# Reading direction and byte positions of matmul operands in an attention and gated-MLP kernel

## The chip, the cores and the metric

The kernel runs on one core of one Trainium2 chip. The metric is the device time of one execution, in microseconds (us). A profile of one execution stands beside it; its span runs from the first to the last instruction.

## The reference

The input x has 2048 rows of 512. It is layer-normalised, and the result goes two ways. One is attention with 32 heads of 16 columns, in which each row looks at 8 earlier rows, two apart; the other is a two-layer MLP with a hidden width of 1792 and a squared ReLU. The MLP's output, through a SiLU, gates that of the attention.

```python
xn = _layernorm(x, axis=-1)
# attention: qkv = xn @ wqkv; each row attends to rows s, s-2, ..., s-14; then @ wo
s = _A_ref(xn, A_wqkv, A_wo)
# MLP: h = relu(xn @ w1 + b1) ** 2; out = h @ w2 + b2
g = _silu(_B_ref(xn, B_w1, B_b1, B_w2, B_b2))
return x + s * g
```

## The kernel before

**The products.** TensorE does four kinds of product, and each of them is a run of matmuls of a 128x128 stationary operand, which a weight load brings in, with a moving operand of 512 columns. All operands are split into a high and a low float32r part, and each product is the sum of three passes (PASSES, line 34): high by high, high by low, low by high. So a product over 512 rows of input is 4 x 3 = 12 matmuls into one PSUM bank. Every matmul has a weight load of its own.

- `qkv` (line 477) makes q, k and v: the stationary operand is a part of xt, the normalised and transposed x of one tile of 128 rows; the moving operand is a row block of wqkv (`wq`). In the profile: `pq<-wq,xt`, or `pq<-wq,xT` for the first four tiles, which lie in xT.
- `up` (line 509) makes one block of 128 hidden columns for a chunk of 512 rows: stationary w1 (in `w12[f]`), moving four pieces of 128 columns of x. In the profile: `ph<-xT,w` for the first chunk, `ph<-xU,w` for the others, whose x parts are read back from memory.
- `down` (line 653) multiplies h by w2: stationary 128 columns of h, moving 512 columns of w2, which lies in the same buffer as w1. For each of four tiles of 128 rows, three matmuls are added into the bank `pb[j]`. In the profile: `pb<-w,h`.
- `out_product` (line 689) multiplies the attention's output by wo: stationary oT, moving wot. In the profile: `pw<-wot,oT`.

**The stages.** First the weights and the first tiles of x are loaded and split. Then comes the qkv stage, tile pair by tile pair (lines 598 to 645), in which VectorE begins the attention, which it computes without TensorE. Then come four chunks of 512 rows (lines 721 to 817): for each f, one `up` of 12 matmuls and one `down` of 12, with out products and the gate in between. The attention runs along on VectorE; two running sums of estimated time, one for TensorE and one for VectorE (`clock`, line 57), decide while the program is built how much of it is put between two products. Each engine's instructions are kept in the order in which they are written.

**Where the operands lie.** A tile's place in a partition follows from the sizes of the tiles before it. In the kernel before, the parts that are read as moving operands (wq, w12, xT, xU, wot) all begin 480 bytes past a multiple of 512, and so do the stationary parts in w12, h, oT and xT: one matmul's stationary part is 128 float32r numbers, 512 bytes, and parts follow each other in whole multiples of 512 bytes. Only the tiles xt (`place`, line 444; buffers of pool pxT), which are the stationary operands of `qkv` from the fifth tile on, begin 384 bytes past a multiple of 512. Below, the distance of a matmul is the place of the stationary part that is loaded while it runs, less the place where its moving operand begins, modulo 512 bytes. It is 416 in those `qkv` products and 0 in nearly all others.

Of the kernel before, what the change touches and what calls it, by code (L numbers as in the profile page):

```python
# [8 lines left out]
F32 = mybir.dt.float32  # L9
FR = mybir.dt.float32r  # L10
# [4 lines left out]
P = 128  # L15
# [37 lines left out]
def body(ctx: ExitStack, tc: tile.TileContext, x, wqkv, wo, w1, b1, w2, b2, out):  # L53
# [32 lines left out]
    PE, V, A, G = Ordered(nc.tensor, "PE"), Ordered(nc.vector, "V"), Ordered(nc.scalar), Ordered(nc.gpsimd)  # L86
# [12 lines left out]
    hpool = ctx.enter_context(tc.tile_pool(name="ph", bufs=1))  # L99
    psum = ctx.enter_context(tc.tile_pool(name="psum", bufs=1, space=bass.MemoryType.PSUM))  # L100

    def psA(name):
        return psum.tile([P, 512], F32, name=name, tag="acc", bufs=4)

    def psH(name):
        return psum.tile([P, 512], F32, name=name, tag="h", bufs=2)
# [22 lines left out]

    p1ctx = ExitStack()  # L130
    px, pstg, pxT = (p1ctx.enter_context(tc.tile_pool(name=n, bufs=1)) for n in ("px", "pstg", "pxT"))
    xins = {}


# [238 lines left out]
    w12 = {}  # L373
# [19 lines left out]
    mv, means, rs, shifts, xn, xb, pTs, xt, xT, seen = ({} for _ in range(10))  # L393
# [108 lines left out]
    def load_xT(c):  # L502
        xT[c] = xTa.tile([P, TPC, 2, KT, P], FR, name=f"xU{c}", tag="xT")
        for j in range(0, TPC, 2):
            A.dma_start(xT[c][:, j:j + 2].bitcast(F32), sx[c][:, j:j + 2])
# [3 lines left out]
    def up(c, f):  # L509
        ph = psH(f"ph{c}_{f}")  # L510
        n = 0
        for kt in range(KT):
            for a, b in PASSES:
                PE.matmul(ph.rearrange("p (j n) -> p j n", n=P), w12[f][:, a, 0, kt * P:(kt + 1) * P],
                          xT[c][:, :, b, kt, :], start=n == 0, stop=n == 11)
                n += 1
        if f == NF - 1 and c + 1 < NCH:
            load_xT(c + 1)
        h = hpool.tile([P, 2, 512], FR, name=f"h{c}_{f}", tag="h", bufs=3)
        A.activation(ph, ph, AF.Relu, bias=b1t[:, f:f + 1])  # L520
        A.activation(h[:, 0], ph, AF.Square)
        A.activation(ph, ph, AF.Square)
        hs[f] = h, ph, clock["PE"] + 2000
# [74 lines left out]
    for a in range(2, NT, 2):  # L598
        b, more, later = a + 1, a + 2 < NT, a + 6 < NT
# [20 lines left out]
        if not more:  # L620
            up(0, 0)
# [8 lines left out]
        if not more:  # L630
            pump()
            up(0, 1)
            lowh(0)
# [16 lines left out]
    p2 = ctx.enter_context(tc.tile_pool(name="p2", bufs=1))  # L650
    pws, gs = {}, {}

    def down(pb, f, j):
        h, w = hs[f][0], w12[f]
        for n, (a, b) in enumerate(PASSES):
            PE.matmul(pb[j], h[:, a, j * P:(j + 1) * P], w[:, b, 1, :],
                      start=f == 0 and n == 0, stop=f == NF - 1 and n == 2)


# [2 lines left out]
    oqs, oTs = {}, {}  # L662
# [13 lines left out]
    def trans_o(t, pT):  # L676
        src = pT.rearrange("p (g n) -> p g n", g=4)
        V.transpose(out=src.rearrange("p g (b n) -> p b g n", n=32),
                    in_=oqs[t // 2][:, :, t % 2].rearrange("p b (g c) -> p b g c", c=32))
        oTs[t] = p2.tile([P, 2, 4, P], FR, name=f"oT{t}", tag="oT", bufs=2)  # L680
        A.activation(oTs[t][:, 0], src, AF.Copy)
        seen[t] = src, clock["V"] + 800

# [37 lines left out]
    for c in range(NCH):  # L721
        last = c == NCH - 1
        pb = [psA(f"pb{c}_{j}") for j in range(TPC)]
        t0 = c * TPC
        room = ROOM if c else ROOM0
        for f in range(2, NF):
            if c == 0:
                next_w()
            up(c, f)
            pump()  # L730
            if c == 0 and f == 3:
# [6 lines left out]
            if c == 0:  # L738
                if 6 <= f < 10:
                    split(wot[:, 0, f - 6], wot[:, 1, f - 6], rwo[(f - 6) // 2][:, (f - 6) % 2], G)  # L740
            elif f == 2:
                finish(t0 - 4, G)
            elif f == 3:
                finish(t0 - 3, G)
                load_r(t0 - 2)
                load_r(t0 - 1)
                trans_o(t0 - 2, psT(f"pT{t0 - 2}"))
                trans_o(t0 - 1, psT(f"pT{t0 - 1}"))
            elif f == 4:
                lowo(t0 - 2)  # L750
                lowo(t0 - 1)
            elif f == 5:
                out_product(t0 - 2, psT(f"pw{t0 - 2}"))
            elif f == 6:
                finish(t0 - 2, G)
                out_product(t0 - 1, psT(f"pw{t0 - 1}"))
            elif f == 7:
                finish(t0 - 1, G)
# [6 lines left out]
            if f == 10:  # L765
                for i in range(2):
                    trans_o(t0 + i, psT(f"pT{t0 + i}"))
# [5 lines left out]
            if not (last and f == NF - 1):  # L773
                for j in range(TPC):
                    down(pb, f - 2, j)
# [6 lines left out]
        if not last:  # L782
            for i in range(2):
                for j in range(TPC):
                    down(pb, NF - 2 + i, j)
                if i == 0:
                    pump(room)
# [10 lines left out]
        else:  # L798
# [7 lines left out]
            for j in range(TPC):  # L806
                for f in range(NF - 3, NF):
                    down(pb, f, j)
                gate(c, j, pb)
                if j < 2:  # L810
                    finish(t0 + j, V, xl[:, j])
            for j in range(2, TPC):
                n = D // 2 if j == TPC - 1 else D
# [25 lines left out]
```

## Time and profile before

| | us |
|---|---|
| median of 3 runs | 501.99 (501.86 to 504.11) |
| span of the profiled execution | 500.6 |
| TensorE busy in it | 491.6 |
| VectorE busy in it | 422.9 |
| ScalarE busy in it | 212.2 |
| GpSimd busy in it | 133.4 |

The profiled execution's own time is the span and what lies around it; the median of the runs is 1.4 us over the span. In the profile PE is TensorE's matmuls and PEld its weight loads, DVE is VectorE, ACT ScalarE, POOL GpSimd, SP the queue that starts most DMAs. Since a helper records every operation, nearly all rows have its line, L82, and are told apart by their tiles. The duration of one matmul in the profile is longer than the time from its start to that of the next, since matmuls overlap; the pace of a run of matmuls is read from the chain of work that ended last, which gives the start and the length of a run and the count in it.

### The profile page before, as it was taken

The numbers are of one execution on the slowest core, as the hardware profiler recorded it, in microseconds if no ns is written. First come the engines' busy times: TensorE is split into PE (matmuls) and PEld (weight loads), VectorE is DVE, ScalarE is ACT, GpSimd is POOL, SyncE is SP. The second block draws the span as 40 slices with busy tenths as digits, with TensorE's granted clock in tenths as the row PEclk, the third lists the DMA queues.
The fourth block names the chain that finished last, engine by engine and source line by source line (L and its number), as shares of the span: only waits on it lengthen the run. The fifth ranks groups of instructions, "written<-read, shape, count | busy, mean of one in ns | idle before, by whom it ended". The sixth has DMA issues, their size and how long they took to land.

```text
span 500.6 us, 5874 instructions
## 1 busy us (share of the span) xinstructions
PE 491.6 (98%) x2154; PEld 402.8 (80%) x2154; DVE 422.9 (84%) x352; ACT 212.2 (42%) x377; POOL 133.4 (27%) x123
## 2 busy tenths in 40 slices
PE   8997999999999999999999999999999999999997
PEld 6876888888888888888888888888888888888886
DVE  5905599999889699997999998899999889996235
ACT  5526556652344465515424342441254256214331
POOL 1312255343427499200223002041300022220000
PEclk9998999999999999999999999999999999999999
DMA  8996989969966975644216416152333705121022
GB/s 292 283 287 187 324 293 332 289 200 331 310 234 236 206 252 140 201 168 158 101 26 241 156 44 259 67 216 68 117 126 97 269 2 199 43 84 64 22 84 85
DMA packets 48520, 88.79 MB, mean 177 GB/s; under 512 B 5372, under 2 KB 32364, under 8 KB 45676
## 3 DMA queue, kind: packets, MB, share of 16 engines
q1 hardware_dynamic: 44172, 54.87, 35.1%
q10 hardware_dynamic: 4320, 33.56, 18.8%
q8 instruction: 17, 0.28, 0.2%
q14 instruction: 11, 0.09, 0.0%
HBM read 57.94 MB, written 27.32 MB: 170 GB/s over the span
## 4 chain that ended last, share of the span: by engine, by line
PE 95%; DMA 3%; ACT 0%; DVE 0%; SPq 0%; issue 0%; POOL 0%; ACTq 0%; POOLq 0%
PE ph L82 30%; PE pb L82 30%; PE pq L82 25%; PE pw L82 9%; DMA xb<-xn 2%; DMA x<-in_A_x 1%; PE pxT L82 0%; SPq L455 0%; ACT scratch L82 0%; DVE z L82 0%; ACT xn L82 0%; DVE st L82 0%; POOL rs L82 0%; ACT stg L82 0%; DVE xn L82 0%
## 5 line engine op out<-in xcount | busy, mean ns | idle before, releaser
L82 PE MATMUL pb<-w,h 128*128 128x512 f32 x672 | 160.6, 389 | 0.0
L82 PEld LDWEIGHTS pb<-w,h 128*128 128x128 f32 x672 | 126.1, 188 | 26.2
L82 PE MATMUL ph<-xU,w 128*128 128x512 f32 x504 | 120.6, 389 | 0.0
L82 PEld LDWEIGHTS ph<-xU,w 128*128 128x128 f32 x504 | 94.6, 188 | 19.6
L82 ACT ACTIVATE ph<-ph,b1t 128x512 f32<-128x512 f32 x56 | 37.0, 660 | 159.6 <-PE ph L82 150.6
L82 PE MATMUL pq<-wq,xt 128*128 128x512 f32 x432 | 101.3, 395 | 0.0
L82 PEld LDWEIGHTS pq<-wq,xt 128*128 128x128 f32 x432 | 81.1, 188 | 19.7
L82 DVE TENSOR_TENSOR pr<-k,q 128x2048 f32<-128x2048 f32 x32 | 77.6, 2425 | 1.6 <-DMA q<-sq 1.2
L82 DVE TENSOR_TENSOR pv<-v,L 128x2048 f32<-128x2048 f32 x32 | 74.2, 2320 | 0.6
L82 DVE TENSOR_REDUCE L<-pr 128x128 f32<-128x2048 f32 x32 | 72.9, 2278 | 0.6
L82 DVE TENSOR_REDUCE v<-pv 128x256 f32<-128x2048 f32 x32 | 72.9, 2279 | 0.6
L82 DVE TENSOR_TENSOR h<-ph,h 128x512 fp32r<-128x512 f32 x56 | 38.0, 679 | 31.9 <-ACT ph L82 31.9
L82 PE MATMUL pw<-wot,oT 128*128 128x512 f32 (+1 forms) x204 | 45.9, 376 | 0.0
L82 POOL TENSOR_TENSOR z<-z,xr 128x512 f32<-128x512 f32 x12 | 25.5, 2127 | 67.1 <-DVE z L82 57.7
L82 PEld LDWEIGHTS pw<-wot,oT 128*128 128x128 f32 x204 | 36.8, 188 | 7.1
L82 ACT ACTIVATE stg<-pq 128x512 f32<-128x512 f32 x48 | 28.2, 593 | 31.4 <-PE pq L82 28.0
L82 POOL TENSOR_TENSOR w<-w1r,w 128x512 fp32r<-128x512 f32 x14 | 29.4, 2098 | 44.9 <-ACT w L82 40.0
L82 PE MATMUL ph<-xT,w 128*128 128x512 f32 x168 | 40.5, 390 | 0.0
L82 PEld LDWEIGHTS ph<-xT,w 128*128 128x128 f32 x168 | 31.5, 188 | 6.7
L82 PE MATMUL pq<-wq,xT 128*128 128x512 f32 x132 | 32.7, 408 | 3.6 <-ACT stg L82 3.6
L82 ACT ACTIVATE h<-ph 128x512 fp32r<-128x512 f32 x56 | 33.7, 602 | 1.8
L82 PEld LDWEIGHTS pq<-wq,xT 128*128 128x128 f32 x132 | 25.5, 196 | 10.3 <-ACT stg L82 4.1
(64 smaller groups left out, 330.4 us busy)
## 6 DMA issues: line engine op xcount, KB each, us to landing
k<-sk ACTq DMA_DIRECT2D x8, 1408.0 KB, 8.3
v<-sv ACTq DMA_DIRECT2D x8, 1408.0 KB, 6.5
sx<-xt SPq DMA_DIRECT2D x12, 512.0 KB, 6.2
xU<-sx ACTq DMA_DIRECT2D x6, 1024.0 KB, 8.6
x<-in_A_x SPq DMA_DIRECT2D x16, 256.0 KB, 4.5
sk<-stg SPq DMA_DIRECT2D x8, 512.0 KB, 4.5
sq<-stg SPq DMA_DIRECT2D x8, 512.0 KB, 5.8
q<-sq ACTq DMA_DIRECT2D x8, 512.0 KB, 9.0
```

The source lines that it names most:

```text
L82: return tc.keep_in_program_order(f(*a, **k))
```

## The change

Four things are changed.

1. Every `down` product reads its moving operand from the last column to the first, and writes its output columns in the same order, so that each result lands where it did.
2. Every `up` product with an odd f does the same, over its four pieces and within each; those with an even f are as before.
3. A tile of 56 numbers (224 bytes) is put ahead of the xt buffers, with a GpSimd memset that writes it.
4. The tile that holds h is 1056 numbers wide in place of 1024, of which the first 1024 are used as before; the tile that holds oT is 1040 wide, of which 1024 are used from the 2nd number on (even tiles) or from the 4th (odd tiles).

```diff
     px, pstg, pxT = (p1ctx.enter_context(tc.tile_pool(name=n, bufs=1)) for n in ("px", "pstg", "pxT"))
+    G.memset(pxT.tile([P, 56], F32, name="gap"), 0.0)
...
             for a, b in PASSES:
-                PE.matmul(ph.rearrange("p (j n) -> p j n", n=P), w12[f][:, a, 0, kt * P:(kt + 1) * P],
-                          xT[c][:, :, b, kt, :], start=n == 0, stop=n == 11)
+                to, x_ = ph.rearrange("p (j n) -> p j n", n=P), xT[c][:, :, b, kt, :]
+                if f % 2:
+                    to, x_ = to[:, ::-1, ::-1], x_[:, ::-1, ::-1]
+                PE.matmul(to, w12[f][:, a, 0, kt * P:(kt + 1) * P], x_, start=n == 0, stop=n == 11)
...
-        h = hpool.tile([P, 2, 512], FR, name=f"h{c}_{f}", tag="h", bufs=3)
+        full = hpool.tile([P, 1056], FR, name=f"h{c}_{f}", tag="h", bufs=3)
+        h = full[:, :1024].rearrange("p (a n) -> p a n", a=2)
...
-            PE.matmul(pb[j], h[:, a, j * P:(j + 1) * P], w[:, b, 1, :],
+            PE.matmul(pb[j][:, ::-1], h[:, a, j * P:(j + 1) * P], w[:, b, 1, ::-1],
                       start=f == 0 and n == 0, stop=f == NF - 1 and n == 2)
...
-        oTs[t] = p2.tile([P, 2, 4, P], FR, name=f"oT{t}", tag="oT", bufs=2)
+        full = p2.tile([P, 1040], FR, name=f"oT{t}", tag="oT", bufs=2)
+        at = 2 + 2 * (t % 2)
+        oTs[t] = full[:, at:at + 1024].rearrange("p (a g n) -> p a g n", a=2, g=4)
```

With the new sizes the places are these. The three buffers of h, which take turns by f, grow by 384 bytes together, and begin 480, 96 and 224 bytes past a multiple of 512, which is 0, 128 and 256 bytes past where w12's parts begin. The 384 bytes and the 224 of the new tile move xt from 384 to 480, so that its distance is 0. wot moves to 352; the parts of oT begin at 360 (even tiles) and 432 (odd tiles), at distances of 8 and 80 from wot.

TensorE, VectorE, ScalarE and SyncE have the same instructions in the same order as before. GpSimd has one more, near its beginning. Before, the rows from where the identity matrix for the transposes is made:

```order
masks.py:197 MEMSET ident 128x128
masks.py:199 ISA
masks.py:199 AFFINE_SELECT ident<-ident 128x128
L82 MEMSET mhalf 128x1
L82 TENSOR_TENSOR rs_153<-rs_153,mhalf 128x1
```

And now the same place:

```order
masks.py:197 MEMSET ident 128x128
masks.py:199 ISA
masks.py:199 AFFINE_SELECT ident<-ident 128x128
L82 MEMSET gap 128x56
L82 MEMSET mhalf 128x1
L82 TENSOR_TENSOR rs_155<-rs_155,mhalf 128x1
```

The memset of the new tile stands ahead of that of mhalf, the exponent of the layer norm's power; all other rows stand as they did, with other numbers in the names.

## The prediction

> **What bounds the kernel now.** I began with the page: which engine is busy, and the chain of work that ended last.
>
> ```profile
> span 500.6 us, 5874 instructions
> PE 491.6 (98%) x2154; PEld 402.8 (80%) x2154; DVE 422.9 (84%) x352; ACT 212.2 (42%) x377; POOL 133.4 (27%) x123
> PE 95%; DMA 3%; ACT 0%; DVE 0%; SPq 0%; issue 0%; POOL 0%; ACTq 0%; POOLq 0%
> ```
>
> TensorE is busy for 98% of the span and makes 95% of the chain. The waits of TensorE's own queue say the same: it stands still for somebody three times, 5.2 us in all, and all of it early.
>
> ```profile
> PE pq L82 <- ACT stg L82: 3.6, 1, 3.6
> PE warm L82 <- POOL mhalf L82: 1.3, 1, 1.3
> PE pxT L82 <- DVE xn L82: 0.3, 1, 0.3
> ```
>
> So what one matmul takes, times their number, is the time. The groups of matmuls, the count behind the x:
>
> ```profile
> L82 PE MATMUL pb<-w,h 128*128 128x512 f32 x672 | 160.6, 389 | 0.0
> L82 PE MATMUL ph<-xU,w 128*128 128x512 f32 x504 | 120.6, 389 | 0.0
> L82 PE MATMUL pq<-wq,xt 128*128 128x512 f32 x432 | 101.3, 395 | 0.0
> L82 PE MATMUL pw<-wot,oT 128*128 128x512 f32 (+1 forms) x204 | 45.9, 376 | 0.0
> L82 PE MATMUL ph<-xT,w 128*128 128x512 f32 x168 | 40.5, 390 | 0.0
> L82 PE MATMUL pq<-wqraw,scratch 128*128 128x512 f32 x8 | 3.9, 607 | 0.0
> ```
>
> Their 389 ns overlap, so the pace has to come from the chain in order of time: start, length, and the count of instructions in a piece. First its piece in the qkv stage, asked for the window from 45 to 138 us:
>
> ```profile
> 44.92 93.29 PE pq L82 x400
> ```
>
> That is 93.29 / 400 = 233.2 ns from one matmul to the next. Then the chain of the whole span, where the stages meet and at the end:
>
> ```profile
> 142.84 2.80 PE pq L82 x12
> 145.64 2.77 PE ph L82 x12
> 148.41 5.60 PE pq L82 x24
> 154.01 2.76 PE ph L82 x12
> 156.77 2.72 PE pb L82 x12
> 159.49 2.72 PE ph L82 x12
> ...
> 477.73 5.44 PE pw L82 x24
> 483.17 8.16 PE pb L82 x36
> 491.32 5.60 PE pw L82 x36
> ```
>
> `up`, `down` and out products go at 2.72 / 12 = 226.7 ns. A qkv product on the xt tiles takes 5.60 / 24 = 233.3 ns, and does so between two ups, so that it isn't the stage that makes it slow. What sets these products apart is the distance: 416 bytes between the stationary part being loaded and the moving operand being read, against 0 in the others. I take 6.6 ns (233.2 less 226.7) as the price that the trace shows of a distance other than 0.
>
> The last row gives one more number. Of its 36 matmuls 24 have 256 columns in place of 512. The twelve full ones take 2.72 us, so the 24 take 2.88, 120.0 ns each. Two halves take 240.0 ns and one whole takes 226.7: 13.3 ns belong to each matmul whatever its length, and 213.3 to its 512 columns. The weight load, 188 ns long, runs in the shadow of each matmul:
>
> ```profile
> L82 PEld LDWEIGHTS pb<-w,h 128*128 128x128 f32 x672 | 126.1, 188 | 26.2
> ```
>
> If the two reads get in each other's way, these 13.3 ns are the most that can be won back on each matmul.
>
> **The change part by part.** The sum is made against the span of 500.6 us; the median of the runs, 501.99, is 1.4 us above it, and I carry that over unchanged.
>
> *xt moved to distance 0.* 432 matmuls (`pq<-wq,xt`) go from 233.2 to 226.7 ns: 432 x 6.6 = 2.8 us less. All of it lies on the path if nothing else becomes late in that stage. The busy times of the stage, and of the chunks after it:
>
> ```profile
> 45.00:138.00 93.00, 93.00 (x400) 74.88 (x399) 84.76 (x64) 47.75 (x98) 39.48 (x44) 1.00 0.92 295
> 156.00:482.00 326.00, 326.00 (x1440) 269.95 (x1439) 291.29 (x220) 131.27 (x220) 78.70 (x43) 1.00 0.41 138
> ```
>
> The columns are PE, PEld, DVE, ACT, POOL, then the granted clock, and the DMA's share and rate. The stage would shrink to 400 x 226.7 = 90.7 us; VectorE's 84.8 still fit. The DMA engines are at 0.92 there, so a transfer could become late next; that would take back at most these 2.8 us. A page of the Trainium skill speaks against any gain here: "TensorE: Matmul & The Clock Gate", in its step-by-step account of a matmul, says that weights and moving operand come through two read ports of their own, so that loading weights takes nothing from the running matmul. By it the sum has 0 in place of 2.8; the row at 148.41 us doesn't bear it out.
>
> *Down products from the last column.* 672 matmuls on which no row of the trace shows a reversed read. Below, the bound is the fixed part: 672 x 13.3 = 9.0 us less. Above, the farthest row is that of the eight fp32 matmuls (`pq<-wqraw,scratch`): two for each product of 512 columns, and 607 ns long against 389, 218 ns more. It is how long a matmul takes when its operand streams at half the speed, and it would be 146 us more. The row that I take is the nearest, the pace of matmuls whose two reads do not start side by side: 6.6 ns more, 672 x 6.6 = 4.4 us. Two reasons: the h buffers now lie at distances 0, 128 and 256, so two thirds of these matmuls are off the position at which every fast row stands; and the remaining third, at 0, has its reads cross in another order than any row shows.
>
> *Odd up products from the last column.* 4 chunks x 7 products x 12 = 336 matmuls at distance 0, the bounds per matmul as above: from 4.5 us less to 73 us more. With the same row, 336 x 6.6 = 2.2 us more. This is the least certain term: if only the distance counts, it is nothing.
>
> *oT at distances 8 and 80.* 204 matmuls, read forwards: from 13.3 ns less each (2.7 us) to 218 more (44 us); the nearest row, a forward read off distance 0, gives 204 x 6.6 = 1.3 us more.
>
> *The rest.* One more memset on GpSimd, 224 bytes wide per partition, ahead of the exponent that the first layer norm needs. The nearest row is that of another memset, and what it stands beside is VectorE's wait for the first x:
>
> ```profile
> L82 POOL MEMSET mask<- 128x64 f32 x1 | 0.4, 422 | 0.0
> L82 DVE BATCH_NORM_STATS2 st<-x 128x6 f32<-128x512 f32 x6 | 4.1, 687 | 3.5 <-DMA x<-in_A_x 3.5
> ```
>
> It takes 0.4 us while VectorE waits 3.5 us for its first input, so it costs nothing; without that cover it would cost 0.4. The wider tiles change no count of elements, and no engine gets a new wait. Where TensorE's pace changes, the others follow, since their work in the chunks (VectorE 291 of 326 us) fits in either way.
>
> Sum: -2.8 + 4.4 + 2.2 + 1.3 = +5.1 us. The span becomes 505.7, the time 507.1 us, 1.0% more.
>
> **The rivals.** What decides is the pace of the 1008 reversed matmuls. The other two terms give -2.8 + 1.3 = -1.5 us, which is 1.5 ns on each of the 1008. A measurement of this kernel can tell about 0.5%, 2.5 us, from no change. So reversed matmuls below 225.7 ns make it faster, above 230.7 slower, and between them the same.
>
> *The reversed read clears the weight load (faster).* If the fixed 13.3 ns is the two reads meeting in the same part of the memory, two reads that no longer meet lose all of it: 1008 x 13.3 = 13.4 us less, with the -1.5 a time of 487.1. For it: the pace depends on the distance at all, so reads do meet. Against it: the 13.3 ns are the same in all rows at distance 0, for 512 columns in one run (`pb`) and in four (`ph`), as something would be that belongs to each matmul whatever it reads. The Trainium skill ("TensorE: Matmul & The Clock Gate", on why a gap is 56 and not 53.3 ns) gives about 2.5 ns that stay with each warm matmul; by that, 10.8 ns could be won, and the time would be 489.6. No run here shows that split.
>
> *Direction makes no difference.* The reversed matmuls stay at 226.7 ns, because only the start of the stationary part against the lowest byte of the moving part counts, or because only the read of xt was ever slow. Then the time is 501.99 - 2.8 = 499.2, or 500.5 if oT pays its 1.3. For it: nothing in the rows speaks of direction, and `up` with its four separate pieces goes as fast as `down`.
>
> *The reads run in step.* If the weights are read towards lower addresses, a reversed moving read goes the same way, four times 128 columns in 213 ns while the load of 128 lasts 188. The faster one catches up with the slower and stays behind it until the load ends. At three distances a quarter of 512 bytes apart some h buffers would be spared and others not. Taking one to two more times the fixed part for each reversed matmul, 13.3 to 26.7 ns, gives 13.4 to 26.9 us more, and with the -1.5 a time of 513.9 to 527.4. Against it: nothing in the trace shows a matmul that is held for long.
>
> *A reversed read streams at half speed.* The operand, or the output in PSUM, is fetched in lines, and going down uses them badly. At 218 ns more for each, 1008 make 220 us: 720 us. Against it: neighbouring numbers are still used one after another. The Trainium skill ("SBUF — State Buffer", on the first door, its note on cachelines) says that a 16-byte line needs two uses or more for full speed and that any PSUM pattern that isn't contiguous slows matmuls much; whether a step of -1 counts as contiguous, no run here shows.
>
> *The change does nothing.* The 6.6 ns are something else of the qkv products, and neither place nor direction counts: 502.0. It is the case in which the rule of two read ports holds; the rows at 142.84 and 148.41 us, slower in between fast ones, leave it little.
>
> **How the numbers follow.** The forecast (507.1) has a chance of 0.29; its own range reaches from 503.4, where distance 0 costs the odd ups and a third of the downs nothing, to 513.7, where reversed matmuls pay twice 6.6 ns. The other cases: reads that clear each other 0.22, no difference by direction 0.24, reads in step 0.15, half speed 0.06, nothing at all 0.04. The range from 486.5 to 520.0 holds the forecast, the first two rivals, the last, and the lower half of the reads in step: 0.29 + 0.22 + 0.24 + 0.04 + 0.07 = 0.86. What it leaves out are the two cases of long holding. Faster by over 0.5%: 0.22 and half of 0.24, the half in which oT pays nothing, 0.34. Within 0.5%: the other half and the last case, 0.16. Slower: 0.29 + 0.15 + 0.06 = 0.50.
>
> **What would show each step.** In the chain of the changed kernel the piece of qkv products should read 2.72 us for 12, 5.44 for 24; if it still reads 5.60, place wasn't the cause. A piece of 12 down products reads 2.72 now and 2.80 by the forecast; 2.56 where the reads clear each other, and more than 2.88 where they run in step, with pieces of different f unlike each other, since the h buffers take turns. Odd and even ups side by side give the price of direction alone at distance 0. Out products should read 2.80. The forecast is wrong if downs stay under 2.71 us for 12, and wrong the other way if any stage shows TensorE waiting for somebody for microseconds that it doesn't wait for now.

## The result, and the profile after

The changed kernel takes 508.26 us (median of 4 runs, 507.07 to 508.92), the kernel before 502.85 (501.86 to 504.11). The ratio is 1.0113, with a 95% interval of 1.0086 to 1.0141: 1.1% slower. The profiled execution spans 506.0 us against 500.6, 5.4 us more. One run of the experiment on the places alone, further down, took 828.38 us at a granted clock of 0.558, where the other runs of the experiments have 0.97 or more, and is left out of the median and the ratio.

First the head of the page and its chain, by engine:

```profile
span 506.0 us, 5875 instructions
PE 496.9 (98%) x2154; PEld 403.2 (80%) x2154; DVE 423.1 (84%) x352; ACT 212.3 (42%) x377; POOL 134.5 (27%) x124
PE 95%; DMA 3%; ACT 0%; DVE 0%; SPq 0%; issue 0%; POOL 0%; ACTq 0%; POOLq 0%
```

TensorE still makes 95% of the chain, and is busy for 5.3 us more; no other engine's sum moved by more than 1.1. Its waits are what they were, so that the time went into the matmuls themselves:

```profile
PE pq L82 <- ACT stg L82: 3.2, 1, 3.2
PE warm L82 <- POOL ident masks.py:199: 1.3, 1, 1.3
PE pxT L82 <- DVE xn L82: 0.4, 1, 0.4
PE pq L82 <- ACT scratch L82: 0.2, 1, 0.2
```

Now the chain in order of time (start, length, what, how many). First the long qkv piece of the kernel before:

```profile
40.31 99.76 PE pq L82 x420
```

And the changed kernel, the same piece and the pieces from 142 us on:

```profile
39.95 97.11 PE pq L82 x420
...
142.50 2.81 PE ph L82 x12
145.31 5.45 PE pq L82 x24
150.76 2.72 PE ph L82 x12
153.48 2.81 PE pb L82 x12
156.29 2.80 PE ph L82 x12
159.09 2.80 PE pb L82 x12
161.89 2.74 PE ph L82 x12
164.63 2.84 PE pb L82 x12
167.47 2.80 PE ph L82 x12
170.27 2.80 PE pb L82 x12
173.07 2.73 PE ph L82 x12
...
482.39 5.55 PE pw L82 x24
487.94 8.41 PE pb L82 x36
496.35 5.63 PE pw L82 x36
```

Before, a qkv piece of 24 read 5.60 and all pieces of up, down and out products 2.72 for 12. Now qkv reads 5.45, every down 2.80 to 2.84, every odd up (the first `ph`, and those at 156.29 and 167.47) 2.80 or 2.81, the even ups between reversed downs 2.73 or 2.74, and out products 2.78. In the qkv stage the piece of 420 matmuls has gone from 99.76 to 97.11 us, and no wait has come in its place.

The terms: qkv -2.65 in the long piece and -0.15 in the one of 24; 672 downs by 7.2 ns (233.9 ns from the start of one to that of the next, against 226.7), +4.8; 28 odd ups by 0.08, +2.2; 28 even ups by 0.015, +0.4; 15 pieces of out products of 512 columns by 0.055, +0.8. Together +5.4 us, by which the span grew too.

### The profile page after: what moved, and what is told of

It is laid out like the page before. It is cut to its first block, busy times and chain, and to the rows that moved or that the text cites. A ratio compares the mean times of both kernels' runs of the same rounds, so it can differ in the third digit from the quotient of the medians.

```text
span 506.0 us, 5875 instructions
## 1 busy us (share of the span) xinstructions
PE 496.9 (98%) x2154; PEld 403.2 (80%) x2154; DVE 423.1 (84%) x352; ACT 212.3 (42%) x377; POOL 134.5 (27%) x124
## 4 chain that ended last, share of the span: by engine, by line
PE 95%; DMA 3%; ACT 0%; DVE 0%; SPq 0%; issue 0%; POOL 0%; ACTq 0%; POOLq 0%
PE pb L82 31%; PE ph L82 31%; PE pq L82 24%; PE pw L82 9%; DMA xb<-xn 2%; DMA x<-in_A_x 1%; PE pxT L82 0%; SPq L456 0%; ACT scratch L82 0%; DVE z L82 0%; ACT xn L82 0%; DVE st L82 0%; POOL rs L82 0%; ACT stg L82 0%; DVE xn L82 0%
## 5 line engine op out<-in xcount | busy, mean ns | idle before, releaser
L82 PE MATMUL pb<-w,h 128*128 128x512 f32 x672 | 165.5, 398 | 0.0
L82 PE MATMUL ph<-xU,w 128*128 128x512 f32 x504 | 122.7, 394 | 0.0
L82 PE MATMUL pq<-wq,xt 128*128 128x512 f32 x432 | 98.4, 389 | 0.0
L82 POOL TENSOR_TENSOR w<-w1r,w 128x512 fp32r<-128x512 f32 x14 | 31.7, 2264 | 41.6 <-ACT w L82 41.6
L82 POOL TENSOR_TENSOR L<-L,mx_None 128x512 f32<-128x512 f32 x7 | 15.5, 2216 | 71.5 <-DVE mx_None L82 71.5
```

The source lines that it names most:

```text
L82: return tc.keep_in_program_order(f(*a, **k))
```

## The experiments

The forecast was close, but its reason for the largest term was the place of h, not the direction of the read, and the change mixes the two. Theory **direction**: a moving operand that is read from its last column costs 6.7 ns a matmul, wherever the weights lie. Theory **distance**: only the places cost, as they did with xt. The pace figures "from start to start" below are means over the matmuls of one kind, taken from the start times of the single instructions in the trace; all others are pieces of the chain.

### xt alone

```diff
+    G.memset(pxT.tile([P, 24], F32, name="gap"), 0.0)
```

> Of the four parts of the change only the place of xt: a tile of 24 numbers ahead of it moves it from 384 to 480 bytes past a multiple of 512, and h, oT and all reading directions are as before. Both theories (the direction of the moving read costs; the distance of the two reads costs) expect a piece of 12 qkv products to take 2.72 us in place of 2.80 and the kernel to be 2.8 us faster, a ratio of 0.9944. A theory in which the qkv stage is held by something else than its matmuls expects the pace to fall and the time to stay, with new waits of TensorE in that stage.

Measured: 498.91 us (median of 6 runs) against 501.65, a ratio of 0.9931 (0.9905 to 0.9958); the span is 497.8. The chain:

```profile
40.24 97.11 PE pq L82 x420
145.51 5.44 PE pq L82 x24
```

The xt products now go at 5.44 / 24 = 226.7 ns, and the span is shorter by 2.8 us, as both theories had it. This is the one part of the change that helps, and alone it beats both kernels. It also settles what the prediction weighed: the Trainium skill ("TensorE: Matmul & The Clock Gate", the step-by-step account of a matmul) has weights and moving operand come through separate read ports, so that one takes nothing from the other. Here nothing but the place of the weights was moved, and 432 matmuls became 6.6 ns faster each; in float32r, on this chip, the measurement decides against the second half of that rule. Whether the ports are separate it doesn't show.

### The reversal alone

The diff is that of the change in `up` and `down`; no tile is wider, h and oT lie at a distance of 0, and xt at 416.

> Only the reversal of all down products and of the odd up products; every tile lies where it did before. Theory direction: each reversed matmul takes 233.3 ns whatever the distance, so 12 down products take 2.80 us, odd ups 2.80, even ups 2.72 but for their first matmuls, and the kernel is 1008 x 6.7 = 6.7 us slower, a ratio of 1.013. Theory distance (only stationary parts that do not lie where the moving operand begins cost): down and odd up stay at 2.72 us for 12 and the time doesn't change, ratio 1.000.

Measured: 509.61 us (median of 4 runs) against 501.65, ratio 1.0145 (1.0114 to 1.0177). Pieces of its chain in the second chunk:

```profile
242.45 2.80 PE ph L82 x12
245.25 2.80 PE pb L82 x12
248.05 2.73 PE ph L82 x12
250.78 2.81 PE pb L82 x12
253.59 2.80 PE ph L82 x12
256.39 2.73 PE pw L82 x12
```

The ratio that theory direction expected, 1.013, lies in the interval, and the span is 507.4 us, 6.8 more than before. Every down and every odd up is slow (2.80), though all their places are the fast one; even ups and out products keep their pace but for a hundredth. Theory direction holds, theory distance fails for reversed reads. From start to start the 672 downs take 233.5 ns here, against 226.7.

### The places alone

The diff is that of the change without the `::-1`: the tile ahead of xt, the wider h and oT.

> Only the places: the tile ahead of xt, the wider h and oT; every moving operand is read forwards. Theory direction says nothing of down products that are read forwards at distances of 128 and 256; if distance costs them what it cost xt (6.6 ns), two thirds of 672 pay 3.0 us, oT pays 1.0 and xt gives back 2.8: ratio 1.002. If the distance is harmless to down products, the kernel is 1.8 us faster, ratio 0.996. With both prices standing side by side (theory distance plus direction, added up) the changed kernel's reversed downs at 128 and 256 should have been at 240 ns, which they were not; so one of the two prices must be missing here or must not add.

Measured: 502.87 us (median of 9 runs) against 501.65; the ratio is 1.0002 (0.9974 to 1.0030), and that of the two medians, 1.0024, lies inside its interval. Of the two results expected, 0.996 is outside the interval and 1.002 inside it, but the chain shows that the reason given for 1.002 isn't right either; the h buffers take turns:

```profile
267.40 2.72 PE pb L82 x12
270.12 2.73 PE ph L82 x12
272.84 2.80 PE pb L82 x12
275.64 2.75 PE ph L82 x12
278.39 2.72 PE pb L82 x12
281.11 2.72 PE ph L82 x12
283.83 2.72 PE pb L82 x12
286.55 2.73 PE ph L82 x12
289.28 2.80 PE pb L82 x12
```

Only every third down is slow. From start to start, reads forwards take 227.5 ns at distance 0, 227.1 at 256, and 232.9 at 128: a distance of 256 is as good as 0, so that a third of the downs pay and not two thirds. Out products take 230.3 (distance 8) and 231.4 ns (distance 80). So places cost 1.5 us in downs (a third of 56 pieces by 0.08), some 0.8 in out products and about as much in the ups and downs that follow a slow product, and the 2.8 us of xt pay for it.

### Read or write

In the changed kernel a reversed matmul reads w2 backwards and writes PSUM backwards. First the read alone:

```diff
-            PE.matmul(pb[j], h[:, a, j * P:(j + 1) * P], w[:, b, 1, :],
+            PE.matmul(pb[j], h[:, a, j * P:(j + 1) * P], w[:, b, 1, ::-1],
```

> The down products read w2 from the last column but write their output columns forwards, so that the columns of the down products come out mirrored; all else is as before. If the reversed read costs, 12 down products take 2.80 us (233.3 ns each); if the reversed write into PSUM costs, they take 2.72 us (226.7 ns); if each has a share, something between.

Then the write alone:

```diff
-            PE.matmul(pb[j], h[:, a, j * P:(j + 1) * P], w[:, b, 1, :],
+            PE.matmul(pb[j][:, ::-1], h[:, a, j * P:(j + 1) * P], w[:, b, 1, :],
```

> The down products read w2 forwards but write their output columns from last to first, so that the columns of the down products come out mirrored; all else is as before. With the read alone reversed a down product took 233.6 ns. If the write costs nothing, 12 take 2.72 us here (226.7 ns); if read and write share a price that isn't added when both are reversed, they take 2.80.

Measured: 507.18 us and 501.74 us, one run each, beside runs of the kernel before of 501.65 (median) and 501.88. A down piece of the one and of the other:

```profile
271.64 2.81 PE pb L82 x12
```

```profile
269.86 2.72 PE pb L82 x12
```

All of it is the read (233.6 ns from start to start, against 226.7 with the write reversed). For the write, the prediction had left open whether a step of -1 counts as contiguous in the sense of the Trainium skill's note on cachelines ("SBUF — State Buffer", first door): by the pace of 226.7 ns it does.

### Which step backwards costs

The moving operand of `up` is four pieces of 128 columns, 4096 bytes apart. Here the two directions are parted, by f:

```diff
+                if f % 4 in (1, 2):
+                    to, x_ = to[:, :, ::-1], x_[:, :, ::-1]
+                if f % 4 in (1, 3):
+                    to, x_ = to[:, ::-1], x_[:, ::-1]
```

> Only the up products, in four kinds by f modulo 4: 0 reads forwards, 1 reads its four pieces and each piece from last to first (as the changed kernel's odd ones), 2 reads the pieces in order but each from its last column, 3 takes the pieces from last to first but reads each forwards. Results land where they did. If the direction from one number to the next is what costs, kinds 1 and 2 take 233.3 ns and kinds 0 and 3 take 226.7. If the way the whole operand is walked costs (its start at the far end), kinds 1 and 3 are the slow ones.

Measured: 504.5 us, one run. The ups with f of 5, 6, 7 and 8 of the second chunk, which are kinds 1, 2, 3 and 0:

```profile
251.70 2.81 PE ph L82 x12
...
259.96 2.81 PE ph L82 x12
...
268.22 2.72 PE ph L82 x12
...
273.66 2.72 PE ph L82 x12
```

Kinds 1 and 2 are slow, 3 and 0 are fast: 233.6 and 233.6 ns against 226.7 and 226.9. What costs is to go from one number to the one before it. To take whole pieces of 512 bytes in falling order is free.

### All distances, forwards and backwards

Two kernels put the stationary parts elsewhere in each f, in steps of 32 bytes for h and of 4 for oT:

```diff
+        full = hpool.tile([P, 1144], FR, name=f"h{c}_{f}", tag="h", bufs=3)
+        at = 8 * ((c * NF + f) % 16)
+        h = full[:, at:at + 1024].rearrange("p (a n) -> p a n", a=2)
...
+        full = p2.tile([P, 1032], FR, name=f"oT{t}", tag="oT", bufs=2)
+        at = t % 8
```

> All reads forwards; the stationary parts of down lie at distances of 0 to 480 bytes in steps of 32, another in each f, and those of the out products at 0 to 28 bytes in steps of 4 past where the buffer begins; xt stays at 416. Theory period: the down products repeat after 256 bytes, with 226.7 ns at 0 and 256, 233 at 128 and 384, and no distance below 226.7, since 13.3 ns belong to each matmul. Rival: the 13.3 ns are the two reads meeting, and some distance gives a pace of 224 ns or less.

> The same places, with all down and all out products read from the last column. Theory direction: about 233.4 ns at 0 and 256, at most 2 ns more elsewhere, in no place below 231. Theory reads in step: the pace rises and falls by over 10 ns with the distance, and some distance gives less than 226.7 ns, so that the change would only have picked bad places.

The second kernel has the same places, with `::-1` in `down` and in `out_product`. In both, the wider tiles also move xt, to a distance of 320 and not the 416 named above, and the buffers of `w12` for f of 11 to 13, which begin 448 bytes past a multiple of 512 and not 480.

Measured: 505.91 us and 510.74 us, one run each. Means of the downs from start to start, in ns, 22 to 76 matmuls each:

| distance | 0 | 32 | 64 | 96 | 128 | 160 | 192 | 224 |
|---|---|---|---|---|---|---|---|---|
| forwards | 228.2 | 233.0 | 233.4 | 234.1 | 232.9 | 233.5 | 230.3 | 233.4 |
| backwards | 234.4 | 233.3 | 233.2 | 233.5 | 236.6 | 233.7 | 233.2 | 233.2 |

| distance | 256 | 288 | 320 | 352 | 384 | 416 | 448 | 480 |
|---|---|---|---|---|---|---|---|---|
| forwards | 228.5 | 232.8 | 233.5 | 234.4 | 232.2 | 233.0 | 229.1 | 232.8 |
| backwards | 233.8 | 233.2 | 233.1 | 233.4 | 235.0 | 233.5 | 233.3 | 233.2 |

Forwards, the second half of the table repeats the first after 256 bytes; 0 and 256 are the fast places (the mean is over 227 because the first matmuls after a slow product are slow too), 192 and 448 lie in between, and no place has a mean below 226.7. Backwards, the price is there in all places tried, with more at 128 and 384 (236.6 and 235.0 ns). So the rival in which reversed reads run in step with the load, and cost or spare over 10 ns by the place, is out; so is the one in which the change only picked bad ones of these places. One rival is left. A fast place for a reversed read, as narrow as that of a forward one, could lie between the steps: such a read starts at the last number of its row, and in no run do the weights begin there (modulo 256 bytes); the nearest ones begin 4 bytes past it, and are slow.

A step of 8 bytes is enough to lose the fast place: out products read forwards take 226.7 ns at 0 in the kernel before and 230.3 at 8 with the places alone (here 229.1 and 231.3, two products each).

The moved buffers of `w12` tell one thing more: what counts is the place of the weights relative to the moving operand, not the place alone. The forward downs of f 11 to 13, whose w2 begins at 448, are fast when h begins there too, modulo 256 (228.9 ns, 22 matmuls), and take 233.3 ns (15 matmuls) when it begins at 480, which is the fast place of all other downs. The ups with these weights, against x at 480, take 233.4 ns.

### With a shorter weight load

Is the price paid where the moving read meets the read of a weight load? Then a load of fewer columns should cost less.

```diff
+            m = P if f < 4 or f == NF - 1 else 64 if f % 4 < 2 else 32
+            d = slice(None, None, -1 if f % 2 else 1)
+            PE.matmul(pb[j][:m, d], h[:, a, j * P:j * P + m], w[:, b, 1, d],
```

> The kernel with xt alone moved, whose down products for f from 4 to 12 load only the first 64 (f modulo 4 is 0 or 1) or 32 (2 or 3) of each 128 columns of h, so that the other rows of each tile lack those f; with an odd f they read w2 from the last column, with an even one forwards. Theory meeting reads: what a matmul takes over the 213.3 ns of its 512 columns is paid where it meets the read of a weight load, so with half the load about half is paid: 220 ns forwards and 223 reversed for 64 columns, 217 and 218 for 32. Theory fixed: both the 13.3 ns and the 6.7 ns of a reversed read belong to the matmul, so the pace stays at 226.7 and 233.3 whatever the load.

Measured: 501.02 us, one run. The groups of weight loads show that they are shorter (128, 64 and 32 columns: 188, 134 and 108 ns), and the chain gives the downs of f 2 (128 columns, forwards), 3 (128, backwards), 4 (64, forwards), 5 (64, backwards), 6 (32, forwards) and 7 (32, backwards):

```profile
L82 PEld LDWEIGHTS pb<-w,h 128*128 128x128 f32 x240 | 45.1, 188 | 10.6
L82 PEld LDWEIGHTS pb<-w,h 128*64 128x64 f32 x240 | 32.3, 134 | 22.1
L82 PEld LDWEIGHTS pb<-w,h 128*32 128x32 f32 x192 | 20.8, 108 | 22.1
```

```profile
162.00 2.72 PE pb L82 x12
...
167.44 2.81 PE pb L82 x12
...
172.98 2.76 PE pb L82 x12
...
178.46 2.80 PE pb L82 x12
...
183.99 2.78 PE pb L82 x12
...
189.53 2.80 PE pb L82 x12
```

Neither theory has it right. Backwards the pace doesn't depend on the load (2.81, 2.80, 2.80), as the theory fixed said. Forwards it gets worse with a shorter load (2.76, 2.78), which no theory here expected; a shorter load also changes which bytes are read when, so that the place and the length can't be told apart in it.

### With fewer columns

The last run cuts the moving operand instead.

```diff
+            cut = [0, 512] if f < 4 or f == NF - 1 else [0, 256, 512] if f % 4 < 2 else [0, 384, 512]
+            for i, e in zip(cut, cut[1:]):
+                PE.matmul(pb[j][:, i:e][:, d], h[:, a, j * P:(j + 1) * P], w[:, b, 1, i:e][:, d],
```

> The kernel with xt alone moved, whose down products for f from 4 to 12 cut the 512 columns of each matmul in two matmuls, of 256 and 256 (f modulo 4 is 0 or 1) or of 384 and 128 columns (2 or 3), with a weight load each; odd f read from the last column of each part, even ones forwards. What is computed stays the same. At 0.417 ns a column, forwards 256 columns should take 120.0 ns and 384 columns 173.3 (13.3 ns beside the columns). Theory per matmul: a reversed read costs 6.7 ns more whatever its length, so 126.7 and 180.0 ns reversed. Theory per column: the reversed read goes slower all along, by 1 in 32 (13.3 ns in 512 columns) while less than 13.3 stay beside the columns (6.7), so that reversed takes 120.0 ns for 256 columns, no more than forwards, and 176.7 for 384.

Measured: 559.14 us, one run, a time that can't be compared: the builder's running sum counts each part as a whole matmul, so that the attention is spread otherwise and TensorE waits for others. The pace of the parts can. TensorE's timeline of the second chunk, f of 4 and of 5 with 24 halves each (start, length, group):

```profile
286.99 3.04 PE L82 MATMUL pb<-w,h 128*128 128x256 f32 x24
289.86 2.91 PE L82 MATMUL ph<-xU,w 128*128 128x512 f32 x12
292.60 3.00 PE L82 MATMUL pb<-w,h 128*128 128x256 f32 x24
295.44 2.88 PE L82 MATMUL ph<-xU,w 128*128 128x512 f32 x12
```

From start to start of the groups, 24 halves take 289.86 - 286.99 = 2.87 us forwards and 295.44 - 292.60 = 2.84 backwards, 119.6 and 118.3 ns each; over all halves of the run that follow each other without a wait the means are 119.6 (263) and 118.4 ns (184). A price of 6.7 ns for each reversed matmul would have made it 126.7, 3.04 us in all; the theory per column expected no difference at 256. Its other test failed to tell anything: with 384 and 128 columns in turn, both directions took over 220 ns for the longer part, far from either expectation. Long and short part together take 281.7 ns forwards and 281.4 backwards, where two halves take 239 and 237; why, no run here shows.

## Why the prediction was right, point by point

The forecast was 507.1 us and 1.0% more, the result 508.26 and 1.1% more.

- **What bounds the kernel.** TensorE's pace is the time, before and after; no wait took the place of anything, and VectorE and the DMA engines kept up with the faster qkv stage, as the busy times of that stage had it.
- **xt, -2.8 us.** Measured -2.8 in the chain, and shown by itself: 0.9931, its interval holding the 0.9944 that was expected.
- **Downs, +4.4 us.** Measured +4.8. The size is right and most of the reason is wrong. The prediction put two thirds of it down to the places of h. But 256 is as good as 0, and a reversed read pays its 6.7 ns at every place tried, so that the wider h added next to nothing: 234.7 ns at 128 against 233.6 at 0 and 233.4 at 256. Its other reason, that the reversed reads at distance 0 might pay as much for another order, is what happened to all of them. It was taken from the pace of a different thing, a forward read at a bad place, which happens to cost the same 6.6 ns. That the two sizes agree is luck, as far as the runs go: none shows one cause for both.
- **Odd ups, +2.2 us.** Measured +2.2; "if only the distance counts, it is nothing" was the case that failed.
- **oT, +1.3 us.** Measured +0.8: 180 full matmuls pay some 4.7 ns and not 6.6, and the 24 short ones nothing.
- **Not foreseen, +0.4 us.** The first two matmuls of a forward product after a reversed one are slow as well (238.4 and 231.6 ns in the even ups, then 226.7), so that even ups read 2.73 or 2.74.
- **The rivals.** The fixed 13.3 ns were not won back by any place or direction tried. That direction makes no difference is refuted by the reversal alone; reads in step by the scan, in steps of 32 bytes; half speed by 233 ns where it would have been 445; and that nothing counts by xt alone.

What stays open is the cause inside the chip. The price comes from the read alone, from steps of one number downwards, in all places tried; a shorter load doesn't lower it, and halves of 256 columns don't pay it. That fits a read that goes slower all along while something else, worth as much at 256 columns, is saved; it is argued from one run, not shown.

## What to carry to other kernels

Where TensorE is the chain, read the pace of one matmul from pieces of the chain and compare it between product kinds; here a difference of 6.6 ns between two kinds was worth 0.6% of the span and took one small tile to remove. In these runs the fast place of a float32r stationary part is a multiple of 256 bytes from where the moving operand begins. Leave moving operands in rising order within each run of numbers; here the order of whole runs of 512 bytes and the direction of the output cost nothing. And when a change mixes a gain with a loss, time the parts alone: the part worth keeping was hidden under two that cost more.

## What the runs showed that was not expected

The distance counts modulo 256 bytes, not 512: reads forwards take 227.1 ns at 256, 232.9 at 128 and 227.5 at 0 in one kernel. The fast place is narrow, lost at 8 bytes for out products and at 32 for downs. A shorter weight load made forward matmuls slower, 2.76 and 2.78 us for 12 against 2.72. And a PSUM output written from its last column costs nothing, 2.72 us for 12.
